# Landmark products that trail by ten steps, an attention batch that starts in the planned head, and weight work placed elsewhere

## The chip, the cores and the metric

The program runs on one core of a Trainium2 chip. TensorE (PE) does the matmuls; VectorE (DVE), ScalarE (ACT) and GpSimd (POOL) do the work between them; SyncE (SP) issues the DMAs. The metric is the device time of one execution in microseconds; the median of the runs shown counts.

## The reference

Attention is approximated with 32 landmarks for each head (means over 18 neighbouring tokens), and two dense layers follow:

```python
# q, k, v: (4 batches, 8 heads, 576 tokens, 64)
q_lm, k_lm = means of q and k over groups of 18 tokens
A, Bm, C = sm(q, k_lm), sm(q_lm, k_lm), sm(q_lm, k)
Z = Bm^T / (norms);  six times: Z = 2 * Z - Z @ Bm @ Z
x = A @ Z @ C @ v                      # then as 2304 x 512
h = x @ w_in;  x = (h * sigmoid(h)) @ w_out           # layer 1, d_ff 2048
h = x @ w_in2; out = (h * tanh(log1p(exp(h)))) @ w_out2   # layer 2
```

The four weight matrices come as float64; the kernel turns them into float32 on the chip. A product of float32 quality is made of three matmuls: each operand is split into a rounded part (hi) and a rest (lo), and hi*hi, hi*lo and lo*hi are added up.

## The kernel before, in words

**Landmark products.** Attention's last factor is never formed. For each batch a small matrix `wt` (from Z, C and v) is multiplied with w_in: eight landmark products `u_steps(b, jp)`, each for two of the 16 column tiles of w_in. Then h = uw x ath, where `ath`, `atl` are the parts of the softmax of the queries.

**The head.** Batch 0 and 1's attention, the conversion of layer 1's weights, layer 1 of batch 0 (`h_stream`, `y_stream`) and the landmark products of batch 1 are generators. The planner `interleave` orders them: each step has costs by engine, dependencies and a delay, and the step with the lowest beginning plus delay goes next. What it orders is issued in that order on every engine; later code can fill gaps. `y_stream` has two turns over the 16 row tiles of w_out; in the second one `wsplit_stream(j)` may split tile j into hi and lo (an ACT copy at line 794 and a DVE subtraction at line 797), with a delay of 7.32.

**The loop over layer 1.** 96 steps t follow: i from 2 to 7 (halves of batches 1 to 3, 288 tokens) and j from 0 to 15. A step has six h matmuls, the SiLU (tanh on ACT, product on DVE, hi on ACT, lo on POOL at line 662) and, two steps later, twelve y matmuls. Between them `advance` takes steps of the attention of the batch to come, 2 x 2.4 in a step of i = 2 and 2 x 1.8 later (`RA`, `RB`). That attention has to be complete at j = 1 of a batch's second half; then one landmark product follows every other step. `convert2` makes float32 of layer 2's weights and stores them in DRAM, one tile every other step from t = 0 (a load, a clip on POOL, two ACT and two DVE operations, a store). The scheduler under the kernel follows this order as a priority and takes ready work from later steps where an engine is free.

**The last half and layer 2.** From t = 80 the first tokens of layer 2 are loaded, and from t = 84 `second_weights` loads and splits its weights, one tile of each matrix in a step: ACT copies hi, DVE subtracts (line 605). Twelve turns of each lie in layer 1, six in the first steps of layer 2, where POOL subtracts. The lo parts of w_in2 go into the tiles `g0` to `g7`, which hold the landmark products until the last half has read them. A step of layer 2 is twelve hh matmuls of 384 columns and nine o matmuls of 512; six DVE operations of Mish lie between (`z` at lines 1025 to 1028), ACT's exponentials and POOL's lo part (line 1032).

**Banks.** PSUM has eight: y uses 0 to 3, h 5 and 4 in turn, attention and landmark products of the loop 6 and 7.

Of the kernel before, what the change touches and what calls it, by code (L numbers as in the profile page):

```python
# [9 lines left out]
F32R = mybir.dt.float32r  # L10
# [9 lines left out]
P = 128  # L20
# [3 lines left out]
RA = 2.4  # L24
RB = 1.8
# [19 lines left out]
def interleave(streams, done):  # L45
# [4 lines left out]
    for gen, enter, delay in streams:  # L50
        enter()
        step = next(gen, None)
        if step is not None:
            live.append([delay, gen, enter, step, 0.0])
    while live:
        best = None
        for s in live:
            step = s[3]
            if any(d not in done for d in step.deps):
                continue  # L60
            t = max([s[4]] + [done[d] for d in step.deps])
            begin, idle = None, 0.0
            for e, c in step.cost:
                at = max(t, free.get(e, 0.0))
                if begin is None:
                    begin = at
                else:
                    idle += max(0.0, at - max(begin, free.get(e, 0.0)))
                t = at + c + LATENCY
            score = (t if begin is None else begin) + WASTE * idle + s[0]  # L70
            if best is None or score < best[0]:
                best = (score, s, t)
        assert best, [(s[0], s[3].deps) for s in live]
        _, s, _ = best
        step = s[3]
        t = max([s[4]] + [done[d] for d in step.deps])
        for e, c in step.cost:
            t = max(t, free.get(e, 0.0)) + c
            free[e] = t
            t += LATENCY  # L80
        s[4] = t
        if step.key is not None:
            done[step.key] = t + (DMA_LATENCY if step.key[0] in LOADED else 0.0)
        s[2]()
        s[3] = next(s[1], None)
        if s[3] is None:
            live.remove(s)
# [3 lines left out]
def nystrom_moe_kernel(ctx, tc, q, k, v, w1i, w1o, w2i, w2o, out):  # L91
# [6 lines left out]
    M = 32  # L98
# [379 lines left out]
    def attn_softmax(st):  # L478
# [3 lines left out]
        perm = b not in dve_tr  # L482
        eng, on, c = (pool, "pool", 1.3) if perm else (dve, "dve", 0.7)
# [5 lines left out]
        yield Step([(on, c)])  # L489
        eng.tensor_tensor(ta, ta, mx[:, 0][:, :, None].to_broadcast([P, G, M]), op=ALU.subtract)  # L490
# [6 lines left out]
        yield Step([(on, c)])  # L497
        eng.tensor_tensor(ta, ta, mx[:, 2][:, :, None].to_broadcast([P, G, M]), op=ALU.mult)
# [212 lines left out]
    def attn_batch(b):  # L711
        for g in range(2):
# [150 lines left out]
    streams += [(u_steps(1, jp), Banks((3, 7)[jp % 2]), 1.24) for jp in range(NF // 2)]  # L863
    streams += [(wsplit_stream(j), Banks(), 7.32) for j in range(NF)]
# [3 lines left out]
    cur[0] = Banks(6, 7)  # L868
# [24 lines left out]
    cv2 = convert2() if is64 else iter(())  # L893

# [23 lines left out]
    def second_weights(which):  # L918
# [3 lines left out]
        for n in range(NF + 2):  # L922
# [9 lines left out]
            if n >= 2:  # L932
                j = n - 2
                raw = pend.pop(j)
                if which == 0:
                    hi = wp.tile([P, ND, P], F32R, tag=f"wc{j}", name=f"wi2h{j}")
                    if j % 2 == 0:
                        los = wp.tile([P, 2, ND, P], F32R, tag=f"g{j // 2}", name=f"wi2l{j}")
                    lo = los[:, j % 2]
# [21 lines left out]
    bg.append(attn_batch(2))  # L961
    for t in range(len(steps)):
        i, j = steps[t]
        b, hf = i // 2, i % 2
        if hf == 1 and b + 1 < B and j == 1:
            while bg:
                advance()
        if hf == 1 and j == 10 and b + 2 < B:
            bg.append(attn_batch(b + 2))
# [5 lines left out]
        hb = bank(5 - t % 2, f"h{t}")  # L975
# [3 lines left out]
        if hf == 1 and b + 1 < B and j % 2:  # L979
            u_all(b + 1, j // 2)  # L980
        advance(RA if i == 2 else RB)
        if t % 2 == 0 and i < nblk - 1:
            next(cv2, None)
        if i == nblk - 1:
# [4 lines left out]
            if j == 4:  # L989
                wgen = [second_weights(0), second_weights(1)]  # L990
            if j >= 4:
                next(wgen[0], None)
# [3 lines left out]
        advance(RA if i == 2 else RB)  # L996
# [160 lines left out]
```

## Time and profile before

| what | value |
| --- | --- |
| median of 3 runs | 908.48 us (908.18 to 911.49) |
| profiled execution, its time | 903.28 us |
| its span, first to last instruction | 901.5 us |
| PE busy | 858.0 us (95%) |
| DVE, ACT, POOL busy | 652.5, 473.0, 290.5 us |
| head, to the first h of the loop | 187.7 us |
| loop over layer 1 | 187.7 to 482.5 us |
| layer 2 | 482.5 to 901.5 us |

Line numbers (L610) are those of the kernel before. PEclk is the granted share of TensorE's clock: 1.00 is 2.4 GHz, and the lower level is 1.2 GHz. L610 is the helper that issues h, y and hh matmuls, told apart by the tile that they write.

### The profile page before, as it was taken

How to read it: one execution, taken by the hardware profiler on the slowest of the kernel's cores; microseconds unless marked ns; L12 is line 12 of the kernel's file. 1: busy time of each engine (PE TensorE's matmuls, PEld its weight loads, DVE VectorE, ACT ScalarE, POOL GpSimd, SP SyncE). 2: the span in 40 equal slices, each digit the busy share in tenths (PEclk: the TensorE clock that was granted, in tenths of full speed). 3: DMA queues.
4: the chain of work that ended last, by engine and by line, in shares of the span. 5: the costliest groups of instructions: out<-in, count | busy, mean ns of one | idle time of the engine just before them, and what ended most of it. 6: DMA issues, size and time to landing. Idle time of an engine off the chain costs nothing.

```text
span 901.5 us, 15046 instructions
## 1 busy us (share of the span) xinstructions
PE 858.0 (95%) x5440; PEld 756.1 (84%) x5440; DVE 652.5 (72%) x1267; ACT 473.0 (52%) x1013; POOL 290.5 (32%) x332
## 2 busy tenths in 40 slices
PE   7699989969999999999999899999999999999997
PEld 5467767759899898999998789899899999989896
DVE  4888867378795849832365997787787787797776
ACT  4656553255553636644365555555554554555544
POOL 2311332014333435434334742242242242242221
PEclk9999999988999999999999999999999999999999
DMA  8545664405565363713072310110110110000000
GB/s 240 157 124 167 179 185 110 106 26 157 154 195 147 95 185 119 269 41 94 26 202 71 101 53 1 36 35 1 36 36 1 36 37 1 35 1 1 36 1 35
DMA packets 95354, 79.62 MB, mean 88 GB/s; under 512 B 52528, under 2 KB 80688, under 8 KB 95280
## 3 DMA queue, kind: packets, MB, share of 16 engines
q1 hardware_dynamic: 95280, 78.67, 30.9%
q8 instruction: 42, 0.69, 0.3%
q14 instruction: 32, 0.26, 0.1%
HBM read 60.82 MB, written 17.83 MB: 87 GB/s over the span
## 4 chain that ended last, share of the span: by engine, by line
PE 76%; DVE 10%; DMA 4%; ACT 4%; issue 3%; POOL 2%; SPq 1%; ACTq 0%; DVEq 0%; POOLq 0%
PE hh L610 21%; PE o L1088 20%; PE y L610 13%; PE h L610 6%; PE ya L829 5%; PE u L533 3%; PE ha L630 3%; DMA k<-in_k_dram 1%; PE cv L374 1%; DVE z L1026 1%; DVE wl L797 1%; DVE z L1028 1%; DMA rawt<-in_moe_w_out_dram 1%; PE nw L423 1%; POOL g L662 1%
## 5 line engine op out<-in xcount | busy, mean ns | idle before, releaser
L1032 POOL TENSOR_TENSOR g<-z,g 128x384 fp32r<-128x384 f32 x94 | 96.0, 1022 | 253.0 <-ACT g L1029 251.2
L1088 PE MATMUL o<-wh,g 128*128 128x512 f32 x576 | 166.4, 396 | 8.2 <-ACT g L1029 6.7
L610 PE MATMUL y<-g,wh 128*128 128x288 f32 x768 | 163.3, 303 | 0.6 <-ACT yo L682 0.5
L662 POOL TENSOR_TENSOR g<-g,g 128x288 fp32r<-128x288 f32 x96 | 82.0, 854 | 183.8 <-ACT g L661 142.8
L1088 PEld LDWEIGHTS o<-wh,g 128*128 128x128 f32 x576 | 106.0, 188 | 29.6 <-ACT g L1029 9.8
L610 PEld LDWEIGHTS y<-g,wh 128*128 128x128 f32 x768 | 125.3, 191 | 5.8 <-issue 4.0
L610 PE MATMUL hh<-yh,wi2l 128*128 128x384 f32 x384 | 129.3, 337 | 0.0
L610 PE MATMUL hh<-yh,wi2h 128*128 128x384 f32 x384 | 129.1, 336 | 0.0
L610 PE MATMUL hh<-yl,wi2h 128*128 128x384 f32 x384 | 128.9, 336 | 0.0
L1029 ACT CAST g<-z 128x384 fp32r<-128x384 f32 x96 | 49.3, 514 | 136.3 <-DVE z L1028 136.3
L610 PE MATMUL y<-g,wl 128*128 128x288 f32 x384 | 114.7, 299 | 0.0
L1015 DVE TENSOR_SCALAR e<-hh 128x384 f32<-128x384 f32 x96 | 53.4, 557 | 64.8 <-PE hh L610 64.3
L610 PE MATMUL h<-ath,uw 128*128 128x288 f32 x384 | 94.0, 299 | 5.4 <-DVE g L660 5.4
L660 DVE SCALAR_TENSOR_TENSOR g<-th,h 128x288 f32<-128x288 f32 x96 | 43.1, 449 | 71.1 <-ACT th L659 64.6
L1088 PE MATMUL o<-wl,g 128*128 128x512 f32 x288 | 81.9, 391 | 0.0
L1016 ACT ACTIVATE e<-e 128x384 f32<-128x384 f32 x96 | 50.3, 524 | 51.6 <-DVE e L1015 51.5
L610 PEld LDWEIGHTS hh<-yh,wi2h 128*128 128x128 f32 x384 | 72.1, 188 | 3.9
L610 PEld LDWEIGHTS hh<-yl,wi2h 128*128 128x128 f32 x384 | 72.1, 188 | 3.8
L610 PEld LDWEIGHTS y<-g,wl 128*128 128x128 f32 x384 | 73.3, 191 | 0.6 <-issue 0.6
L1026 DVE SCALAR_TENSOR_TENSOR z<-z,r 128x384 f32<-128x384 f32 x96 | 71.1, 740 | 3.3
L610 PEld LDWEIGHTS h<-ath,uw 128*128 128x128 f32 x384 | 67.8, 190 | 6.7 <-DVE g L660 5.9
L610 PEld LDWEIGHTS hh<-yh,wi2l 128*128 128x128 f32 x384 | 72.1, 188 | 0.0
(168 smaller groups left out, 1611.8 us busy)
## 6 DMA issues: line engine op xcount, KB each, us to landing
rawi<-in_moe_w_in_dram SPq DMA_DIRECT2D x16, 512.0 KB, 5.3
rawo<-in_moe_w_out_dram SPq DMA_DIRECT2D x16, 512.0 KB, 3.9
rawt<-in_moe_w_in_dram SPq DMA_DIRECT2D x16, 512.0 KB, 5.1
w2c<-ct SPq DMA_DIRECT2D x32, 256.0 KB, 3.1
rawt<-in_moe_w_out_dram SPq DMA_DIRECT2D x16, 512.0 KB, 4.8
w2r<-w2c SPq DMA_DIRECT2D x32, 256.0 KB, 2.9
v<-in_v_dram SPq DMA_DIRECT2D x32, 144.0 KB, 3.8
ysc<-yo SPq DMA_DIRECT2D x32, 144.0 KB, 1.9
```

The lines of the kernel that those rows point to most:

```text
L533: pe.matmul(ub[64 * p : 64 * p + 64, jj, g], wt[:, p].rearrange("a h m -> a (h m)"), wc[2 * jp + jj][:, (2 * g + p) * P : (2 * g + p + 1) ...
L610: pe.matmul(o, a, b_, start=first and i == 0, stop=last and i == n - 1)
L630: pe.matmul(hb[:, :HB], uw[j // 2][:, j % 2, g], ath[0][:, g, hf * HB : (hf + 1) * HB], start=g == 0, stop=g == 1)
L660: dve.scalar_tensor_tensor(g2, th, 1.0, hb[:, :HB], op0=ALU.add, op1=ALU.mult)
L662: eng.tensor_tensor(gl, g2, gh.bitcast(F32), op=ALU.subtract)
L829: pe.matmul(yb[hf, m][:, :HB], wof[j][:, m * P : (m + 1) * P], gst[j // 2][:, j % 2, hf], start=j == 0, stop=j == NF - 1,)
L1015: dve.tensor_scalar(e, h, 20.0, None, op0=ALU.min)
L1016: ins = act.activation(e, e, AF.Exp)
L1026: dve.scalar_tensor_tensor(z, z, -2.0, r, op0=ALU.add, op1=ALU.mult)
L1029: act.copy(gh, z)
L1032: eng.tensor_tensor(gl, z, gh.bitcast(F32), op=ALU.subtract)
L1088: pe.matmul(obank[i][c], a[:, c * P : (c + 1) * P], w, start=j == 0 and k == 0, stop=j == NF - 1 and k == 2,)
```

## The change

Softmax of the queries of batches 2 and 3 subtracts and multiplies on POOL, as batches 0 and 1 already did, and no longer on DVE. The attention of batch 2 becomes a spare stream of the planner (delay 8.0), which ends when all other streams are done; what is left goes on in the loop. All of the loop advances 2 x 1.35 steps of attention; it has to be complete at j = 11 of a batch's second half, and the landmark products trail by ten steps: three in the second half of the batch before, five in the first half of the batch that uses them. The splits of w_out have a delay of 2.0. `convert2` starts at t = 14, makes 18 turns up to t = 63 and 16 in the 16 steps after. `second_weights(0)` starts at t = 80 with 5 turns in 4 steps, and 11 of its lo parts get tiles of their own. Banks: h 4 and 6, attention and landmark products 5 and 7, products of batch 1 in 3 and 4.

```diff
--- before.py
+++ after.py
@@ -21,8 +21,8 @@
 PT = 96
 HB = 288
 NC = 6
-RA = 2.4
-RB = 1.8
+RB = 1.35
+SHIFT = 10
 NB2 = 384
 LAG = 2
 LAG2 = 2
@@ -47,12 +47,12 @@
 
     free = {}
     live = []
-    for gen, enter, delay in streams:
+    for gen, enter, delay, *spare in streams:
         enter()
         step = next(gen, None)
         if step is not None:
-            live.append([delay, gen, enter, step, 0.0])
-    while live:
+            live.append([delay, gen, enter, step, 0.0, bool(spare)])
+    while not all(s[5] for s in live):
         best = None
         for s in live:
             step = s[3]
@@ -479,23 +479,21 @@
 
         b, g = st["b"], st["g"]
         u = f"{b}{g}"
-        perm = b not in dve_tr
-        eng, on, c = (pool, "pool", 1.3) if perm else (dve, "dve", 0.7)
         yield Step([("dve", 0.75)], [("ta", b, g)])
         taf = st["ta"]
         ta = taf.rearrange("a (c l) -> a c l", l=M)
         mx = ap.tile([P, 3, G], F32, tag="mx", bufs=2, name=f"mx{u}")
         dve.tensor_reduce(mx[:, 0], ta, axis=AX.X, op=ALU.max)
-        yield Step([(on, c)])
-        eng.tensor_tensor(ta, ta, mx[:, 0][:, :, None].to_broadcast([P, G, M]), op=ALU.subtract)
+        yield Step([("pool", 1.3)])
+        pool.tensor_tensor(ta, ta, mx[:, 0][:, :, None].to_broadcast([P, G, M]), op=ALU.subtract)
         yield Step([("act", 0.68)])
         act.activation(ta, ta, AF.Exp)
         yield Step([("dve", 1.2)])
         dve.tensor_reduce(mx[:, 1], ta, axis=AX.X, op=ALU.add)
         dve.tensor_scalar(mx[:, 1], mx[:, 1], 1e-9, None, op0=ALU.add)
         dve.reciprocal(mx[:, 2], mx[:, 1])
-        yield Step([(on, c)])
-        eng.tensor_tensor(ta, ta, mx[:, 2][:, :, None].to_broadcast([P, G, M]), op=ALU.mult)
+        yield Step([("pool", 1.3)])
+        pool.tensor_tensor(ta, ta, mx[:, 2][:, :, None].to_broadcast([P, G, M]), op=ALU.mult)
         if b == 0:
             yield Step([("dve", 0.77)], (), ("ath", 0, g))
             if 0 not in ath:
@@ -709,6 +707,8 @@
             yield step
 
     def attn_batch(b):
+        if b == 2:
+            yield Step((), [("wt", 1, 1), ("ath", 1, 1)] + [("ci", j) for j in OWN])
         for g in range(2):
             units[b, g] = new_unit(b, g)
             yield from whole_unit(units[b, g], True)
@@ -860,12 +860,14 @@
         streams += [(attn_transposes(units[1, g], ti, 4 + ti), Banks(), (0.75, 0.87)[g]) for ti in range(2)]
         streams += [(second_attention(g), a1, (0.67, 1.15)[g])]
         streams += [(attn_softmax(units[1, g]), a1, (1.36, 0.66)[g])]
-    streams += [(u_steps(1, jp), Banks((3, 7)[jp % 2]), 1.24) for jp in range(NF // 2)]
-    streams += [(wsplit_stream(j), Banks(), 7.32) for j in range(NF)]
+    streams += [(u_steps(1, jp), Banks((3, 4)[jp % 2]), 1.24) for jp in range(NF // 2)]
+    streams += [(wsplit_stream(j), Banks(), 2.0) for j in range(NF)]
+    attn2 = attn_batch(2)
+    streams += [(attn2, Banks(5, 7), 8.0, True)]
     done = {}
     with tc.manual_schedule(engines={act.engine, dve.engine, pe.engine, pool.engine, sp.engine}):
         interleave(streams, done)
-    cur[0] = Banks(6, 7)
+    cur[0] = Banks(5, 7)
 
 
     nblk = NT // HB
@@ -891,6 +893,7 @@
 
     held.append(outs[5])
     cv2 = convert2() if is64 else iter(())
+    cvn = [0]
 
     def open_second():
         rgt.close()
@@ -934,9 +937,10 @@
                 raw = pend.pop(j)
                 if which == 0:
                     hi = wp.tile([P, ND, P], F32R, tag=f"wc{j}", name=f"wi2h{j}")
-                    if j % 2 == 0:
-                        los = wp.tile([P, 2, ND, P], F32R, tag=f"g{j // 2}", name=f"wi2l{j}")
-                    lo = los[:, j % 2]
+                    if j < 11:
+                        lo = pl.tile([P, ND, P], F32R, tag=f"lo{j}", name=f"wi2l{j}")
+                    else:
+                        lo = wp.tile([P, ND, P], F32R, tag=f"g{j - 11}", name=f"wi2l{j}")
                     split(raw.rearrange("p (t f) -> p t f", t=ND), hi, lo, late.get("lo", dve))
                     win2[j] = (hi, lo)
                 else:
@@ -958,42 +962,48 @@
             y_out(ybank[i], i)
 
     steps1 = steps
-    bg.append(attn_batch(2))
+    bg.append(attn2)
     for t in range(len(steps)):
         i, j = steps[t]
         b, hf = i // 2, i % 2
-        if hf == 1 and b + 1 < B and j == 1:
+        if hf == 1 and b + 1 < B and j == SHIFT + 1:
             while bg:
                 advance()
-        if hf == 1 and j == 10 and b + 2 < B:
-            bg.append(attn_batch(b + 2))
+            if b + 2 < B:
+                bg.append(attn_batch(b + 2))
         if i == nblk - 1 and j == 0:
             for _ in cv2:
                 pass
             open_second()
             ycur, yload, ypart = y_load(0, late["pool"])
-        hb = bank(5 - t % 2, f"h{t}")
+            wgen = [second_weights(0), second_weights(1)]
+        hb = bank((4, 6)[t % 2], f"h{t}")
         h1_matmuls(hb, b, j, hf)
         gt["a", t] = gtiles(t, HB)
         silu2(hb, *gt["a", t], f"{t}", pool)
-        if hf == 1 and b + 1 < B and j % 2:
-            u_all(b + 1, j // 2)
-        advance(RA if i == 2 else RB)
-        if t % 2 == 0 and i < nblk - 1:
-            next(cv2, None)
-        if i == nblk - 1:
+        lin = NF * hf + j - NF - 1 - SHIFT
+        if lin >= 0 and lin % 2 == 0 and b + 1 < B:
+            u_all(b + 1, lin // 2)
+        lin += 2 * NF
+        if b > 1 and lin < NF and lin % 2 == 0:
+            u_all(b, lin // 2)
+        advance(RB)
+        if i < nblk - 1:
+            while cvn[0] < min(34, (18 * (t - 11) // 52 if t < 64 else t - 45)):
+                cvn[0] += 1
+                next(cv2, None)
+        else:
             if j < 4:
                 yload(j)
             elif j < 8:
                 ypart(j - 4)
-            if j == 4:
-                wgen = [second_weights(0), second_weights(1)]
+            for _ in range(1 + (j % 4 == 3)):
+                next(wgen[0], None)
             if j >= 4:
-                next(wgen[0], None)
                 next(wgen[1], None)
         if t >= LAG:
             emit_y(t - LAG)
-        advance(RA if i == 2 else RB)
+        advance(RB)
     lft.close()
```

## Rows read from the trace of the kernel before

**Rows 1.** Windows by stage: window, length, busy us (instructions) by engine, PEclk, DMA.

```profile
166.00:187.60 21.60, 21.60 (x180) 15.37 (x180) 7.92 (x15) 6.43 (x11) 0.66 (x2) 1.00 0.16 25
187.60:206.30 18.70, 11.94 (x72) 10.03 (x69) 17.47 (x35) 14.14 (x34) 3.08 (x3) 0.73 0.18 59
...
222.00:443.50 221.50, 218.24 (x1778) 204.51 (x1778) 136.98 (x297) 113.86 (x264) 87.37 (x104) 1.00 0.46 134
443.50:482.50 39.00, 38.89 (x290) 38.41 (x289) 22.49 (x38) 23.42 (x53) 13.66 (x16) 1.00 0.53 151
482.50:523.30 40.80, 34.18 (x176) 29.81 (x175) 34.55 (x44) 22.24 (x45) 25.19 (x20) 1.00 0.31 86
523.30:878.00 354.70, 354.70 (x1784) 320.41 (x1783) 283.56 (x511) 189.78 (x374) 107.40 (x105) 1.00 0.07 21
```

**Rows 2.** Timeline of DVE and of ACT behind the head's last landmark product.

```profile
188.41 0.69 DVE L550 TENSOR_TENSOR uw<-u,uw 128x512 fp32r<-128x512 f32 x1 [0.66 <-ACT uw L548]
...
188.87 8.41 ACT L794 CAST wh<-wl 128x512 fp32r<-128x512 f32 x16
197.17 0.71 ACT L659 ACTIVATE th<-h 128x288 f32<-128x288 f32 x2
```

**Rows 3.** Timeline of PE, 198 to 222: start, us, instruction, idle before and releaser.

```profile
198.91 0.61 PE L610 MATMUL h<-ath,uw 128*128 128x288 f32 x1 [5.37 <-DVE g L660]
...
203.58 0.44 PE L610 MATMUL h<-ath,uw 128*128 128x288 f32 x1
...
206.30 0.30 PE L610 MATMUL h<-ath,uw 128*128 128x288 f32 x1
...
208.68 0.29 PE L610 MATMUL h<-ath,uw 128*128 128x288 f32 x1
...
217.06 2.19 PE L374 MATMUL cv<-v,ct 96*64 96x128 f32 x24 [1.57 <-ACT ct L360]
219.18 0.85 PE L610 MATMUL y<-g,wh 128*128 128x288 f32 x2
...
221.83 0.30 PE L610 MATMUL h<-ath,uw 128*128 128x288 f32 x1
```

**Rows 4.** Timeline of PE, first hh of layer 2's third and ninth step.

```profile
489.94 0.34 PE L610 MATMUL hh<-yh,wi2h 128*128 128x384 f32 x1
...
523.33 0.34 PE L610 MATMUL hh<-yh,wi2h 128*128 128x384 f32 x1
```

**Rows 5.** Timeline of DVE and of POOL in one of these steps.

```profile
506.10 1.61 DVE L1026 SCALAR_TENSOR_TENSOR z<-z,r 128x384 f32<-128x384 f32 x1
507.75 1.55 DVE L1028 TENSOR_TENSOR z<-z,e 128x384 f32<-128x384 f32 x1
...
505.99 1.31 POOL L605 TENSOR_TENSOR wi2l<-w2r,wi2h 128x512 fp32r<-128x512 f32 x1 [0.62 <-ACT wi2h L604]
507.26 1.62 POOL L605 TENSOR_TENSOR wl<-w2r,wh 128x512 fp32r<-128x512 f32 x1
```

**Rows 6.** Tile z, one line: count, ns min/median/max, first and last start.

```profile
L1028 DVE TENSOR_TENSOR z<-z,e x96: 557/558/1553, 491.7 to 893.8; 128x384 f32<-128x384 f32 x96
```

**Rows 7.** Timeline of ACT and of POOL: one undisturbed SiLU, tanh to lo part.

```profile
318.28 0.41 ACT L659 ACTIVATE th<-h 128x288 f32<-128x288 f32 x1 [2.66 <-PE h L610]
...
319.80 0.81 POOL L662 TENSOR_TENSOR g<-g,g 128x288 fp32r<-128x288 f32 x1 [2.94 <-ACT g L661]
```

**Rows 8.** Timeline of PE: one landmark product.

```profile
303.38 1.09 PE L533 MATMUL u<-wc,wt 128*64 128x128 f32 x16
```

**Rows 9.** Timeline of DVE: conversions of layer 2's weights, first and last of eleven.

```profile
352.64 1.01 DVE L601 SCALAR_TENSOR_TENSOR ct<-rawt 128x512 uint32<-128x512 uint32 x1
...
386.01 1.19 DVE L601 SCALAR_TENSOR_TENSOR ct<-rawt 128x512 uint32<-128x512 uint32 x1
```

**Rows 10.** Tile ta: the subtraction of softmax on POOL and on DVE.

```profile
L490 POOL TENSOR_TENSOR ta<-ta,mx x4: 1157/1298/1602, 18.7 to 137.5; 128x576 f32<-128x576 f32 x4
...
L490 DVE TENSOR_TENSOR ta<-ta,mx x4: 749/796/1177, 204.8 to 343.8; 128x576 f32<-128x576 f32 x4
```

## Prediction

> **What bounds the kernel now.** I read the windows by stage first. From the loop's first undisturbed steps to the end of layer 1, PE is busy for 218.24 of 221.50 and 38.89 of 39.00 us, and then in layer 2 for all of 354.70 us [rows 1]. In these stretches nothing that the change moves on DVE, ACT or POOL can show, unless it makes PE wait: at most 3.26 + 0.11 us are to be had there. Matmul counts do not change. So I looked for the windows in which PE does wait or runs slowly. Two stand out: the beginning of the loop (11.94 of 18.70 us busy, PEclk 0.73) and the first nine steps of layer 2 (34.18 of 40.80 us) [rows 1]. The time before 166 us is not touched, since the moved splits and the spare stream both depend on work that ends at about that time.
>
> **First gap, beginning of the loop.** PE issues the first h at 187.7 us and then stops, because h of step 2 needs the bank of step 0. That bank is freed by the SiLU's product, and its tanh sits on ACT behind all 16 copies of the w_out split (188.87 to 197.17) [rows 2]; PE goes on at 198.91 after 5.37 us [rows 3]. Idle time of PE in this window: 18.70 - 11.94 = 6.76 us [rows 1]. Then it runs at the lower clock: the step from 198.91 to 203.58 takes 4.67 and the next 2.72, where the one from 206.30 to 208.68 takes 2.38 [rows 3]. That is 2.29 + 0.34 = 2.63 us. A second, smaller place follows: cv waits 1.57 us at 217.06, and the twelve y matmuls behind it take 2.65 us (219.18 to 221.83) where 12/18 of 2.38 = 1.59 is usual, 1.06 us more [rows 3]. Sum of the losses: 6.76 + 2.63 + 1.57 + 1.06 = 12.0 us.
>
> **Second gap, beginning of layer 2.** A step costs 354.70 us / 85 = 4.175 us when PE is full (1784 matmuls at 21 in a step, [rows 1]). The six steps from 489.94 to 523.33 take 33.39 us [rows 4], 5.57 each; the excess is 33.39 - 6 x 4.175 = 8.3 us. In these steps POOL subtracts two weight tiles (1.31 and 1.62 us), and in just that time DVE's two z operations take 1.61 and 1.55 us [rows 5] against a usual 0.56 [rows 6]. So about 1.0 us of DVE time is lost with each of POOL's two subtractions, and six DVE operations that need some 3.4 us need 5.5 instead, more than PE's step.
>
> **The change, part by part.**
>
> *Splits of w_out at delay 2.0.* Sixteen ACT copies at 8.41/16 = 0.53 us (8.4 us) and sixteen subtractions leave the beginning of the loop [rows 2]. They go where their inputs are read last, between 166.0 and 187.6 us. There ACT is busy for 6.43 and DVE for 7.92 of 21.60 us [rows 1]: with 8.4 more on ACT, and about 0.7 x 16 = 11.2 on DVE (as the subtraction of the same shape at 188.41 [rows 2]), it is 14.8 and 19.1 us. PE is full there and stays the bound. DVE is nearly full; without that cover the two or three last subtractions, 2 us, would trail into the loop.
>
> *New banks.* The first h now uses bank 4, which the last landmark product of batch 1 holds until its DVE subtraction ends: 188.41 + 0.69 = 189.10 in the old trace [rows 2], so h would begin 1.4 us behind 187.7. Then y of step 0 needs the whole SiLU, 318.28 to 320.61 = 2.33 us when undisturbed [rows 7]; two more h groups (2 x 2.38/3 = 1.59) cover all but 0.75. I also allow one stretch at the lower clock, 1.06 us as measured behind the 1.57 us wait [rows 3]. What is left of the 12.0 is 3.2; **gain 8.8 us**. Bounds: 12.0 if attention fills the hole; 4.7 if the 1.4 and 0.75 stay and both clock losses of the larger kind do (2 x 2.63).
>
> *Attention at 2 x 1.35, complete at j = 11; conversion from t = 14.* Batch 2's attention has 83 steps of the generator. The planner will take few, for a delay of 8 puts them behind everything until DVE lies that far behind; 27 loop steps at 2.7 take 73. Its two chains of dependent work (where cv waited) get more room, and conversions no longer load in the first steps. This is counted in the 8.8. Landmark products keep their number; they are made five steps ahead of use (over 12 us). They share banks 5 and 7 with attention for sixteen steps, not six; the most that is to be had in this stretch is the 3.26 us of waits above, and I take as much again as the loss: 0, bounds -3 and +3.
>
> *Conversions, 16 in 16 steps (t = 64 to 79).* These steps hold five landmark products of 1.09 us [rows 8]; with 16 x 2.38 us they last 43.5 us, 2.72 for a conversion. Eleven conversions stand at 352.64 to 386.01, one in 3.34 us [rows 9], while attention ran too. At that rate 16 need 53.4 us: they fit only if some run ahead of their place, as the program order allows where an engine is free. I take +0.5; bounds 0 and 53.4 - 43.5 = +9.9.
>
> *Softmax on POOL.* Eight operations of 1.30 us come to POOL and eight of 0.80 leave DVE [rows 10]. POOL has 134 of 221.5 us free [rows 1]; 10.4 us of work hide there, and cost PE up to 0.5 each (4 us) if every one makes a SiLU's lo part late. DVE's part is a doubtful relief: while POOL reads, a two-input operation on DVE stretches by 1.0 us [rows 5, 6], so eight overlaps cost up to 8.0 against 6.4 saved. It is hidden by DVE's 84 idle us [rows 1] either way: 0. The Trainium skill says the same more strictly (SBUF — State Buffer, section "Who interferes with whom"): a GpSimd operation that reads SBUF and a DVE operation with two SBUF inputs exclude each other for a whole instruction. By that rule alone the move would be a net loss of about 4 us on DVE (an estimate: eight holds of 1.30 less 6.4 saved); the trace agrees in kind, with 1.61 us for a z operation that usually takes 0.56 [rows 5, 6].
>
> *Weights of layer 2.* In before, lo parts of w_in2 had to wait for tiles that the last half still read; with eleven tiles of their own the splits can start in block 6, and the faster turns finish all 16 in layer 1. Six more splits then fall on ACT and DVE in a window where each has over 15 of 39 us free [rows 1]; even at POOL's 1.31 they need 7.9. I take +0.5 (bounds 0 and +3: their two load buffers are shared with the first tokens' and can be late). In return POOL has one subtraction in a step of layer 2's beginning, not two. One of the two stretched z operations gets its 0.56 back, 1.0 us in each of six steps; I take five of them, since PE's waits for something else than DVE stay: **gain 5.0 us**; bounds 2.5 (the one subtraction overlaps both operations in every other step) and 8.3 (none matters).
>
> **The sum.** -8.8 - 5.0 + 0.5 + 0.5 = -12.8 us. Against the profiled execution: span 901.5 to 888.7, its time 903.28 to 890.5. The median of the runs lies 5.2 us above the profiled time, and I carry that over: 908.48 - 12.8 = **895.7 us**. A change under 0.5% (4.5 us) cannot be told from none.
>
> **The rivals.**
>
> 1. *Only the first gap closes.* The two buffers of `second_weights` are also used by the first tokens, so w_in2 lags, and its late splits meet layer 2's first DVE steps. Then -8.8 + 1 and nothing gained behind: about 900.5. For it: the sharing. Against: PE lost 0.11 us in this block while twenty splits ran in it [rows 1], so it bears late ones. Chance 0.14.
> 2. *The gains are eaten.* The planner places the spare stream's transposes directly behind their loads, which it takes to cost nothing; DVE's fixed order stands still behind them and the products' banks stay taken, so the 5.37 us wait returns together with the lower clock (2.63), or conversions at their measured rate take the 9.9 us. -12.8 + 8.0 to 9.9: 903.7 to 905.6, no change. Against: a spare step's delay. Chance 0.11.
> 3. *Slower.* The conversions in block 6 leave a hole in PE in every step, 3.34 - 2.72 = 0.62 us, and several fall together, so that PE's clock drops as it did behind the 1.57 us wait. At the lower level a step takes 4.67, not 2.38 [rows 3]; over 16 steps that is +36.6, less 12.8: about 932. It decides if such holes recur while PE is granted the lower clock for most of the block; half the block would still give 914. Against it: 6.62 us of idle time in layer 2's first 40.8 us left PEclk at 1.00 [rows 1]. Chance 0.06.
>
> **How the numbers follow.** The forecast has 0.69, its own range by its bounds (not all at one end) 888 to 902. Rival 1 ends within it, rival 2 at its upper end and just above. For 8 in 10 I take 887 to 904.5. Faster by over 0.5% means under 904.0: all of forecast but a few parts in a hundred, rival 1 and a share of rival 2: 0.83. Same (904.0 to 913.0): 0.10. Slower: rival 3 and mishaps that I have not named: 0.07.
>
> **What would show it.** In the changed profile the 16 copies and subtractions should stand between 166 and 190 us among landmark products; the first h some 1.4 us behind the last product; no wait over 2 us in the loop's first steps and PEclk under 1.00 there for one short stretch at most. At layer 2's beginning POOL should have one weight subtraction in a step, one z operation near 1.6 and one near 0.56, and steps of 4.2 to 4.7 us. PE's last instruction of layer 1 should come 8 to 10 us earlier. Wrong would be: a long DVE wait on a load in the head, PE waiting for h banks or lo parts between t = 64 and 79, or steps of 5.5 us in layer 2.

## The result, and the profile after

The changed kernel takes 899.75 us (median of 4 runs, 897.20 to 900.45); beside it the kernel before took 909.99 us. The ratio is 0.9883, 95% interval 0.9851 to 0.9914. In a second series it took 898.26 us against 906.78, ratio 0.9889 (0.9857 to 0.9922). So it is faster by 1.1%, 8.5 to 10.2 us; the prediction said 12.8 us and 895.7 us, and its range, 887 to 904.5, holds the time. How the sum came about is another matter: two of its zeros cost some 4 us each, a term of half a microsecond was about 2, and the gain at the beginning of the loop was larger than I took.

The profiled execution took 899.86 us, with a span of 898.1 us. The two profiled executions differ by only 3.4 us, because that of the kernel before lies below its usual time (903.28 us; its medians in these series were 906.78 to 909.99), so I compare stages, not spans.

First the windows by stage of the kernel after: window, length, then busy us and instructions of PE, weight loads, DVE, ACT and POOL, PEclk, DMA share and GB/s.

```profile
157.50:193.00 35.50, 35.50 (x242) 26.36 (x240) 23.96 (x48) 13.51 (x29) 0.00 (x0) 1.00 0.32 63
193.00:212.00 19.00, 18.99 (x135) 16.56 (x134) 12.66 (x29) 8.96 (x24) 9.26 (x10) 1.00 0.39 100
336.00:378.00 42.00, 35.45 (x265) 33.52 (x264) 33.52 (x71) 27.24 (x65) 24.29 (x26) 0.96 0.70 229
378.00:441.00 63.00, 62.98 (x528) 60.07 (x527) 26.02 (x44) 29.56 (x67) 24.21 (x28) 1.00 0.29 95
441.00:460.00 19.00, 15.60 (x104) 15.16 (x103) 9.98 (x19) 11.53 (x27) 5.94 (x7) 0.91 0.55 158
485.30:520.50 35.20, 33.85 (x176) 29.98 (x176) 28.51 (x44) 19.14 (x39) 16.11 (x14) 1.00 0.20 58
```

Set against [rows 1], the beginning of the loop went from 11.94 of 18.70 us busy at PEclk 0.73 to 18.99 of 19.00 at 1.00, and the first eight steps of layer 2 from 40.80 to 35.20 us. But two stretches of the loop that were nearly full before now have holes: 6.55 us idle at 336 to 378, and 3.40 us at 441 to 460, both with PEclk under 1.00.

**The first gap is closed.** The splits of w_out, by line: the copies of ACT and the subtractions of DVE, with ns min/median/max and first and last start.

```profile
L794 ACT CAST wh<-wl x16: 618/622/631, 156.5 to 190.9; 128x512 fp32r<-128x512 f32 x16
L797 DVE TENSOR_TENSOR wl<-wl,wh x16: 650/681/694, 158.4 to 192.4; 128x512 fp32r<-128x512 f32 x16
```

They stood in one block behind the last landmark product before [rows 2]; now they are spread over the second turn of y, which begins at 157.5 us (the first two copies start 1 us ahead of it), and the last subtraction ends as the loop begins. PE's timeline there, against [rows 3]:

```profile
191.98 1.09 PE L531 MATMUL u<-wc,wt 128*64 128x128 f32 x16
193.01 0.40 PE L608 MATMUL h<-ath,uw 128*128 128x288 f32 x1
...
194.00 1.19 PE L465 MATMUL a<-qT,qb 128*64 128x288 f32 x8
195.12 0.40 PE L608 MATMUL h<-ath,uw 128*128 128x288 f32 x1
...
196.11 0.71 PE L307 MATMUL c<-kT,qb 128*64 128x288 f32 x4
...
198.24 0.69 PE L608 MATMUL y<-g,wh 128*128 128x288 f32 x2
```

No row has a wait: attention matmuls of batch 2 (`a`, then `c`) fill the time in which PE would have waited for the first SiLU.

**Layer 2's beginning.** The first hh of its first and of its ninth step, then the z operations by line, and one step of DVE and POOL, against [rows 4 to 6]:

```profile
485.26 0.34 PE L608 MATMUL hh<-yh,wi2h 128*128 128x384 f32 x1
...
520.46 0.34 PE L608 MATMUL hh<-yh,wi2h 128*128 128x384 f32 x1
```

```profile
L1036 DVE SCALAR_TENSOR_TENSOR z<-z,r x96: 557/558/1616, 492.9 to 889.8; 128x384 f32<-128x384 f32 x96
L1038 DVE TENSOR_TENSOR z<-z,e x96: 557/558/560, 493.5 to 890.4; 128x384 f32<-128x384 f32 x96
```

```profile
506.21 1.62 DVE L1036 SCALAR_TENSOR_TENSOR z<-z,r 128x384 f32<-128x384 f32 x1
507.86 0.56 DVE L1038 TENSOR_TENSOR z<-z,e 128x384 f32<-128x384 f32 x1
...
506.10 1.31 POOL L603 TENSOR_TENSOR wl<-w2r,wh 128x512 fp32r<-128x512 f32 x1 [0.62 <-ACT wh L602]
```

POOL has one weight subtraction in a step, beside it one z operation still takes 1.62 us, and the other one never takes more than 0.56.

**The new holes.** PE's waits of the kernel after, at 336 to 378 (three lines) and at 441 to 460 (two lines): who waited for what, us in all, times, longest.

```profile
PE nw L423 <- DVE rv L435: 3.2, 3, 2.3
PE y L608 <- DVE yo L682: 2.6, 1, 2.6
PE y L608 <- POOL g L660: 0.7, 2, 0.5
...
PE y L608 <- ACT g L659: 2.9, 1, 2.9
PE y L608 <- POOL g L660: 0.5, 1, 0.5
```

How the wait of 2.6 us at 348.92 comes about is seen in the timelines of POOL, of ACT, of DVE and of PE:

```profile
344.28 1.45 POOL L513 TENSOR_TENSOR atl<-at,ath 128x576 fp32r<-128x576 f32 x1 [0.88 <-ACT ath L511]
345.69 0.79 POOL L660 TENSOR_TENSOR g<-g,g 128x288 fp32r<-128x288 f32 x1
346.45 1.07 POOL L590 TENSOR_SCALAR rawt<-rawt 128x512 f32<-128x512 f32 x1
...
347.56 0.69 ACT L592 ACTIVATE rawt<-rawt 128x512 f32<-128x512 f32 x1 [1.79 <-POOL rawt L590]
348.12 0.41 ACT L680 ACTIVATE yo<-y 128x288 f32<-128x288 f32 x1
...
344.36 1.40 DVE L344 TENSOR_SCALAR bc<-be,rc 128x32 f32<-128x32 f32 x1
345.68 1.34 DVE L595 SCALAR_TENSOR_TENSOR rawt<-rawt 128x512 uint32<-128x512 uint32 x1
...
348.92 0.50 PE L608 MATMUL y<-g,wh 128*128 128x288 f32 x2 [2.61 <-DVE yo L682]
```

POOL is a chain of attention's lo part, a SiLU's lo part and a conversion's clip. ACT stands 1.79 us at the scaling that needs the clip, and the copy of y that frees a bank is behind it; DVE's copies of y come at 348.32 and 349.05, when two operations are through that took 1.40 and 1.34 us beside POOL's (the medians of their lines are 0.57 and 0.69). None of the three POOL operations is one that the change moved; whether those have a part in this hole is asked below.

### The profile page after: what moved, and what is told of

Same layout as the page of the kernel before. It is cut to its first block, busy times and chain, and to the rows that moved or that the text cites. A ratio compares the mean times of both kernels' runs of the same rounds, so it can differ in the third digit from the quotient of the medians.

```text
span 898.1 us, 15048 instructions
## 1 busy us (share of the span) xinstructions
PE 863.3 (96%) x5440; PEld 762.3 (85%) x5440; DVE 651.1 (73%) x1265; ACT 472.7 (53%) x1013; POOL 293.9 (33%) x334
## 4 chain that ended last, share of the span: by engine, by line
PE 79%; DVE 8%; DMA 5%; ACT 3%; POOL 2%; issue 2%; SPq 1%; ACTq 0%; DVEq 0%; POOLq 0%
PE hh L608 21%; PE o L1098 20%; PE y L608 14%; PE h L608 7%; PE ya L829 5%; PE u L531 4%; PE ha L628 3%; DMA q<-in_q_dram 2%; PE nw L423 1%; DVE z L1036 1%; DMA w2r<-w2c 1%; DMA k<-in_k_dram 1%; PE cv L374 1%; POOL rawt L590 1%; PE c L307 1%
```

## The experiments

Four more series, each beside runs of the kernel before on the same chip; ratios are to those. "Loop" is the time from the first h of step 0 to the first hh of layer 2, "hh" the first eight steps of layer 2, "head" what lies ahead of the loop, all from the profiled execution of each.

| kernel | median us | ratio to before (95%) | head | loop | PE idle in loop | hh |
| --- | --- | --- | --- | --- | --- | --- |
| before, shown above | 909.99 | | 187.7 | 294.8 | 11.7 | 40.8 |
| before again | 908.27 (one) | | 189.7 | 297.3 | 13.1 | 40.8 |
| after | 899.75 | 0.9883 (0.9851 to 0.9914) | 193.0 | 292.3 | 10.1 | 35.2 |
| after again | 898.26 | 0.9889 (0.9857 to 0.9922) | 191.1 | 293.0 | 10.5 | 35.2 |
| before + early splits | 897.09 | 0.9885 (0.9852 to 0.9918) | 194.4 | 284.3 | 2.9 | 41.3 |
| after, splits late | 911.08 | 1.0042 (1.0017 to 1.0067) | 189.1 | 307.0 | 19.7 | 35.2 |
| before + layer-2 weights | 904.51 | 0.9976 (0.9950 to 1.0001) | 189.5 | 295.7 | 13.9 | 35.1 |
| before + both | 893.16 | 0.9838 (0.9810 to 0.9866) | 192.8 | 286.1 | 3.9 | 35.1 |
| before + both + POOL softmax | 897.35 | 0.9878 (0.9849 to 0.9906) | 191.3 | 291.5 | 8.0 | 35.2 |
| after, conversions as before | 900.88 | 0.9913 (0.9887 to 0.9939) | 187.5 | 295.1 | 13.4 | 35.5 |
| after, attention faster | 898.12 | 0.9892 (0.9857 to 0.9928) | 187.8 | 293.9 | 10.4 | 35.2 |
| after, DVE softmax | 891.47 | 0.9824 (0.9788 to 0.9859) | 187.0 | 287.8 | 5.8 | 35.5 |
| after, wt kept | 896.05 | 0.9871 (0.9834 to 0.9909) | 193.8 | 288.7 | 7.4 | 35.2 |
| after, both of these | 889.70 | 0.9797 (0.9760 to 0.9833) | 190.0 | 284.5 | 4.5 | 35.2 |

### The parts alone

The kernel before, unaltered, for the spread of profiled executions:

> The kernel before, unchanged, once more. Theory: the head (to the first h of the loop) differs between executions by several us through its loads and PE's clock, so the changed kernel's head of 193.0 us against 187.7 is not the change's doing; this run's head lies anywhere between 187 and 194 us, and the loop from there to the first hh takes 294 to 296 us as before. Rival: the change itself lengthened the head; then this run shows 187.7 us again, within 1 us.

Its loop took 297.3 us, 2.5 more than in the profile shown and 1.3 above what I expected, so loops of two executions agree within about 1%, and a difference of under 2.5 us between two loops is not read. The last two stretches of 16 steps repeat within 0.6 us.

The splits alone:

```diff
-    streams += [(wsplit_stream(j), Banks(), 7.32) for j in range(NF)]
+    streams += [(wsplit_stream(j), Banks(), 2.0) for j in range(NF)]
```

> The kernel before with the delay of the w_out splits at 2.0 and nothing else. Theory: the first gap is the splits' alone, 9 to 12 us less than before (about 898 to 900), with no wait over 2 us in the loop's first 20 us. Rival: the slower attention, the later conversions and the new banks closed it; then the splits alone bring less than 4 us.

Median 897.09 us: this one number gives as much as the whole change. PE's largest wait of the loop, and then that of layer 2's beginning:

```profile
PE y L610 <- ACT yo L682: 0.7, 1, 0.7
...
PE o L1088 <- ACT g L1029: 4.3, 4, 1.2
```

The loop is 10.5 us shorter than in the first profile of the kernel before, and 13.0 than in the second. Layer 2's beginning still waits, as it should.

The reverse, all of the change without this:

```diff
-    streams += [(wsplit_stream(j), Banks(), 2.0) for j in range(NF)]
+    streams += [(wsplit_stream(j), Banks(), 7.32) for j in range(NF)]
```

> The changed kernel with the splits' delay back at 7.32. Theory: 9 to 12 us slower than the changed kernel, so about as slow as before (907 to 911), with a wait of about 5 us and a lower clock behind the head. Rival: the spare stream fills the gap, and it loses less than 4 us.

911.08 us, slower than the kernel before. The 16 copies stand in front of tanh again, and PE waits for the bank:

```profile
190.27 8.41 ACT L794 CAST wh<-wl 128x512 fp32r<-128x512 f32 x16
198.57 0.71 ACT L657 ACTIVATE th<-h 128x288 f32<-128x288 f32 x2
...
199.62 0.61 PE L608 MATMUL h<-ath,uw 128*128 128x288 f32 x1 [8.00 <-DVE g L658]
```

So everything else in the change together gives nothing, though it saves 5.6 us at layer 2's beginning: it must lose as much elsewhere. Next, layer 2's weights alone:

```diff
-                    if j % 2 == 0:
-                        los = wp.tile([P, 2, ND, P], F32R, tag=f"g{j // 2}", name=f"wi2l{j}")
-                    lo = los[:, j % 2]
+                    if j < 11:
+                        lo = pl.tile([P, ND, P], F32R, tag=f"lo{j}", name=f"wi2l{j}")
+                    else:
+                        lo = wp.tile([P, ND, P], F32R, tag=f"g{j - 11}", name=f"wi2l{j}")
...
+            wgen = [second_weights(0), second_weights(1)]
...
-            if j == 4:
-                wgen = [second_weights(0), second_weights(1)]
-            if j >= 4:
+            for _ in range(1 + (j % 4 == 3)):
                 next(wgen[0], None)
+            if j >= 4:
```

> The kernel before with only the weight work of layer 2 moved (lo tiles of their own, faster turns from j = 0). Theory A: two load buffers alone make the 3.4 us wait with its 1.7 us of lower clock that the changed kernel shows at 445 to 451 us; then layer 2's beginning gains 5.6 us, the last half loses 5, and the time is that of before within 2 us. Theory B: that wait comes from the loads beginning late (425 us, behind the later conversions); here they begin near 403 us, there is no wait over 1 us, and the time is 5 to 6 us less than before.

904.51 us. The gain at layer 2's beginning is there (35.1 us). Steps 64 to 80 took 41.2 us, 2.6 more than before, and the last 16 steps 38.3, no more than before. Theory B has the mechanism right: the first load begins at 404.16 us, and PE's longest wait from 380 us to layer 2 is 0.6 us, though ACT waits for late loads (11.1 us in 12 waits). Its 5 to 6 us did not come: the gain is 2.7, since steps 64 to 80 give back as much. So the last 5 us of the changed kernel's loss at 80 to 96 (43.8 us) come from something that this kernel does not have.

### Where the rest of the change loses

> The changed kernel with one thing put back: one conversion step behind every even step of layer 1, as in the kernel before, in place of the sparse beginning and one at every step from t = 64. Everything else of the change stays. Theory (the dense conversions stand in ACT's and DVE's order beside attention 3 and hold y_out's and SiLU's copies there, and the late conversions also keep the queue of SP from layer 2's loads): the waits of 2.61 and 2.28 us at 348 to 366 and the low clock behind them go, steps 48 to 80 fall from 102.4 us by 6 to 8, the last 16 steps from 43.8 by 2 to 4, layer 2's first eight steps stay near 35.2; 889 to 893 us, a ratio of 0.977 to 0.981 to the kernel before. Rival A (the even pace of attention or its softmax on POOL holds PE there): steps 48 to 80 stay within 2 us of 102.4, ratio 0.986 to 0.990. Rival B (the early conversions cost y_out's end of the first two blocks what they save): gain of 6 or more at 48 to 80, but 3 or more lost at 4 to 48 (136.4 us in the changed kernel).

```diff
-            while cvn[0] < min(34, (18 * (t - 11) // 52 if t < 64 else t - 45)):
-                cvn[0] += 1
+            if t % 2 == 0:
                 next(cv2, None)
```

My theory fell: 900.88 us. Steps 48 to 80 won 2.6 us (99.8 after 102.4) and the last 16 won 1.5, but steps 4 to 48 lost 8.0 (144.4 after 136.4), beside batch 2's attention: rival B, though with a smaller gain than it asked for. PE's waits at 348.92 and 364.40 are gone (its longest in steps 48 to 63 is now 1.5 us), but what that saves is lost elsewhere. And layer 2's first load still began only at 424.38 us, though the last converted tile was sent off at 382 to 386:

```profile
382.08 3.49 SPq L891 DMA_DIRECT2D w2c<-ct  x2
...
424.38 0.32 SPq L910 DMA_DIRECT2D yr<-ysc  x1
```

> The changed kernel with 1.8 background steps for each call, where the change has 1.35, so that attention 2 and 3 end earlier (attention 3 near t = 52 and not 59), ahead of most of the dense conversions; the conversions stay as changed. Theory (the loss at 338 to 378 us is attention 3 together with the dense conversions, not either alone): steps 48 to 64 fall from 57.7 us by 3 to 5, ratio 0.982 to 0.986. Rival A (the conversions alone hold ACT and DVE): no change within 2 us in steps 48 to 80, ratio 0.987 to 0.990. Rival B (a denser attention brings waits of its own in steps 32 to 48, 53.0 us in the changed kernel): those steps rise by 2 us or more.

```diff
-RB = 1.35
+RB = 1.8
```

898.12 us, no change. Steps 48 to 64 took 49.2 us and not 57.7, but 32 to 48 took 63.1 and not 53.0: the work and its waits moved together. At step 50 PE waits only 0.4 us, but 3.2 at step 46. Rival B.

> The changed kernel with the two softmax operations of batches 2 and 3 back on DVE (POOL has them in the change). Theory of the prediction (a cost of 0): ratio 0.985 to 0.991 to the kernel before, steps 32 to 64 (110.7 us in the changed kernel) within 2 us. Rival (POOL's long operations stretch DVE's in the same stretch and delay POOL's clips, and PE waits for both): steps 32 to 64 fall by 3 us or more, and ratio 0.980 to 0.984.

```diff
+        perm = b not in dve_tr
+        eng, on, c = (pool, "pool", 1.3) if perm else (dve, "dve", 0.7)
...
-        yield Step([("pool", 1.3)])
-        pool.tensor_tensor(ta, ta, mx[:, 0][:, :, None].to_broadcast([P, G, M]), op=ALU.subtract)
+        yield Step([(on, c)])
+        eng.tensor_tensor(ta, ta, mx[:, 0][:, :, None].to_broadcast([P, G, M]), op=ALU.subtract)
```

(and the same for the multiplication.) 891.47 us: the rival, not the prediction's zero. The loop is 4.5 us shorter (287.8 after 292.3), 3.7 of them in steps 48 to 64. PE's waits there, 333 to 387, and then ACT's for POOL's clips:

```profile
PE y L610 <- ACT g L661: 2.2, 1, 2.2
PE nw L423 <- DVE rv L435: 0.8, 2, 0.5
...
ACT rawt L594 <- POOL rawt L592: 3.0, 5, 1.2
```

In the changed kernel ACT's waits for the clips in these steps were 7.5 us in 8. The wait of 2.3 us for DVE at 364.40 is gone here, and PE idles 3.0 of 53.9 us where it idled 6.5 of 57.7. But the hole of step 50 (at 348.92 in the changed kernel) is not softmax's: PE waits 2.2 us in that step here too (341.51), now for ACT's g. It stands, with 2.2 to 2.6 us, in all five profiles that have the change's early splits, conversions and pace, on whichever engine softmax is. With the conversions as before, or the attention faster, PE waits under 0.5 us in that step. So the hole takes both, the conversions and the pace.

Is the price of softmax on POOL one of its own, or only in this plan? The early splits and layer 2's weights on the kernel before, without and with the softmax on POOL:

> The kernel before with two parts of the change alone: the delay of 2.0 for the splits of w_out, and the second weights of layer 2 begun at the last block with buffers of their own for their low parts. Attention, landmark products, softmax, banks and conversions are the kernel before's. Theory (the gains at both places add up, and the other parts of the change cost what the second gives): head to layer 2 as with the split alone, first eight steps of layer 2 at 35.2 and not 41.3 us, 1 to 4 us lost at steps 64 to 96; 890 to 895 us, ratio 0.980 to 0.985, 3 to 7 us under the changed kernel. Rival (the losses at the last half are as large as the gain behind it): ratio 0.987 to 0.990, as the split alone.

> The kernel before with the early splits and layer 2's weight work, as in the run of these two parts, and one more part of the change: the softmax operations of batches 2 and 3 on POOL. Attention's pace, landmark products and conversions are the kernel before's. It asks whether POOL's softmax costs something by itself. Theory (it costs only where conversions stand close together beside the end of attention 3, as in the changed kernel): the steps from 4 to 96 take 275.5 us as without it, within 1.5, ratio 0.981 to 0.986. Rival (POOL's 1.3 us operations in front of its clips and lo parts cost PE time anywhere): 2 to 5 us more in steps 4 to 64 (196.5 without it), ratio 0.986 to 0.990.

```diff
-        eng, on, c = (pool, "pool", 1.3) if perm else (dve, "dve", 0.7)
+        eng, on, c = (pool, "pool", 1.3)
```

893.16 us without, 897.35 with; the two ran in different series, and the intervals of their ratios overlap (0.9838 and 0.9878), so the profiles decide. The window from step 4 to the end of the loop, without and with (one row from each of the two profiles):

```profile
203.30:478.90 275.60, 271.69 (x2175) 255.44 (x2174) 179.85 (x380) 147.81 (x344) 108.88 (x126) 1.00 0.47 137
```

```profile
201.80:482.80 281.00, 272.99 (x2174) 257.96 (x2173) 175.59 (x373) 148.51 (x344) 119.30 (x134) 0.99 0.47 135
```

PE idles 8.0 us and not 3.9, and the window is 5.4 us longer, with the plan of conversions and attention as in the kernel before. My theory (no cost here) fell, and the rival held: steps 4 to 64 took 201.6 us after 196.6. So softmax on POOL costs by itself; DVE did get 4.3 us of its time back, and it bought nothing. PE's largest hole there (the run without it waits 0.7 us in that step) can be followed back, over POOL, ACT and PE:

```profile
206.15 1.71 POOL L498 TENSOR_TENSOR ta<-ta,mx 128x576 f32<-128x576 f32 x1
...
209.61 1.46 POOL L515 TENSOR_TENSOR atl<-at,ath 128x576 fp32r<-128x576 f32 x1 [0.80 <-ACT ath L513]
211.01 1.10 POOL L592 TENSOR_SCALAR rawt<-rawt 128x512 f32<-128x512 f32 x1
...
212.15 0.67 ACT L594 ACTIVATE rawt<-rawt 128x512 f32<-128x512 f32 x1 [1.33 <-POOL rawt L592]
...
213.23 2.08 PE L374 MATMUL cv<-v,ct 96*64 96x128 f32 x24 [2.08 <-ACT ct L360]
```

Softmax's multiplication ends at 207.86 us; its transpose (DVE, 208.06) and hi part (ACT, 208.85) follow, then POOL's lo part, and the clip stands behind that one. ACT waits 1.33 us for the clip, and the copy `ct` that PE needs is next in its order (212.72). The price measured in these pairs holds also what the scheduler orders differently when two operations change their engine.

The second loss. In the changed kernel the last landmark product and the first load of layer 2 stand like this (PE, then SP, then ACT, which waits for that load):

```profile
423.98 1.09 PE L531 MATMUL u<-wc,wt 128*64 128x128 f32 x16
...
425.15 0.32 SPq L910 DMA_DIRECT2D yr<-ysc  x1
...
429.03 0.51 ACT L914 CAST yh<-yr 128x384 fp32r<-128x384 f32 x1 [2.97 <-DMA yr<-ysc]
```

The load begins as the product ends. So it does in all twelve profiles that leave `wt` where it is, 0.1 us behind the product, the kernel before included (403.43 after 403.34 us). The tile `wt` that the products read lies in the attention pool, and layer 2's buffers take over the place of that pool. To test it, `wt` moves to a pool that lives to the end of layer 1:

```diff
-            pl, tag = (wp, f"gt{g + 1}") if b == 0 else (ap, f"wt{g}")
+            pl, tag = (wp, f"gt{g + 1}") if b == 0 else (xp, f"wt{g}")
```

> The changed kernel once more, unaltered, for a second profile of it and a ratio beside the two kernels below. Theory (the head, 193.0 us to the first product of step 0 in the profile at hand, varies from execution to execution and has nothing of the change in it): the part from there to the end repeats within 2 us (705.1), and the head may lie anywhere from 187 to 195. Rival (the early splits or the longer live tiles lengthen the head): head at 192 to 195 again. Ratio to the kernel before 0.985 to 0.992.

> The changed kernel with one change: the tiles wt of batches 1 to 3, which the landmark products read, lie in a pool that lives to the end of layer 1, and not in the attention pool whose place layer 2's loads take over. Theory (the loads of the last block wait for that place, which the last landmark product frees at 425 us; now that the products trail by ten steps, this is 20 us later than before): the first load starts at 400 to 410 us and not at 425, the wait of PE for ACT's copy near 450 goes, the last 16 steps of layer 1 fall from 43.8 to 38.5 to 41, and the kernel is 3 to 5 us faster than the changed one beside it. Rival A (the loads wait for the conversions or for their place in SP's order): start stays at 420 or later, time within 2 us. Rival B (two load buffers are the limit wherever the loads start): the start moves, but the last 32 steps (88.5 us) fall by less than 2.

> The same, with the softmax operations of batches 2 and 3 back on DVE as well. Theory (the two losses are apart, one at steps 48 to 64 and one at 80 to 96, and both go): steps 48 to 64 near 54.0, steps 80 to 96 at 38.5 to 41, 7 to 10 us under the changed kernel, ratio to the kernel before 0.977 to 0.981: 886 to 890 us where the kernel before takes 907. Rival (what one saves the other takes back): ratio 0.981 to 0.985, as with the softmax alone.

The first load goes off at 393.25 us and the last 16 steps have no hole at all:

```profile
393.25 0.32 SPq L910 DMA_DIRECT2D yr<-ysc  x1
```

```profile
444.20:482.50 38.30, 38.30 (x290) 38.30 (x289) 18.52 (x33) 20.73 (x48) 13.69 (x16) 1.00 0.38 116
```

They fell from 43.8 and 44.0 us to 38.3; steps 64 to 80 took 2.0 to 2.2 us more (46.7), since the splits now start in them. Net 3.5 us in the last 32 steps (85.0 after 88.5), and 3.6 to 4.3 in the loop. The median, 896.05, is 2.2 us lower, and the intervals of the two ratios overlap; the place of the loss is shown by the profile, its size to the microsecond is not. The load starts earlier than I expected (400 to 410), the median gains less than the 3 to 5 us. With both mended the kernel takes **889.70 us**, ratio 0.9797 (0.9760 to 0.9833): the best of all, 8.6 us under the changed kernel beside it.

**The head.** Its time in the ten profiles with early splits is 187.0 to 194.4 us (mean 190.9), in the four with late ones 187.7 to 189.7 (mean 189.0). But from the second turn of y, with which the early splits begin, to the first h of the loop it is 35.5 us in all fourteen, with PE full. This is the stretch in the kernel before, where no split stands in it; for the kernel after it is the first row of the windows above.

```profile
152.20:187.70 35.50, 35.50 (x242) 26.39 (x241) 13.99 (x33) 7.76 (x16) 1.30 (x2) 1.00 0.37 85
```

What differs lies ahead of that, so the long head in the profile shown is not the splits' work; the two profiles of the kernel before differ by 2.0 us as well.

## Why the prediction came out as it did, by its own steps

**First gap, right, mis-sized: 8.8 predicted, 10.1 to 13.0 measured.** The splits alone give 10.1 us in the medians (897.09 against 907.20) and 10.5 and 13.0 in the loops. I had left 3.2 us of the 12.0 standing: the bank 4 wait (1.4), the SiLU (0.75) and one clock loss (1.06). None is seen in the changed kernel: the first h stands right behind the last product, and the sign "some 1.4 us behind" did not come. PE had attention's matmuls for those moments and, as the order of the rows suggests (the profile leaves tile numbers out), h of step 1 in the other bank. The gain lies near the upper bound, "if attention fills the hole". The experiment with the splits alone reached it with the old banks, so the new banks earned nothing that is seen. The splits did not stand where the prediction put them: counted back from the first h, 9 of the 16 copies ran ahead of the 21.6 us of [rows 1]. So DVE, which it saw "nearly full" with 19.1 of 21.60 us, is busy 23.96 of 35.50. Two slips touch no term: the window of 34.18 of 40.80 us holds eight steps of layer 2, not nine, and by its own terms the lower bound is 4.6, not 4.7.

**Layer 2's beginning, right: 5.0 predicted, 5.6 measured** (35.2 us after 40.8), with just the rows that were named: one subtraction in a step, one z operation at 1.6 and one at 0.56 us.

**The last half, mis-sized: 0.5 predicted for the weights and 0 for the landmark products, about 2 and 3.6 to 4.3 measured.** Early weight work by itself costs 1.9 us in steps 64 to 96 (79.0 after 77.1 with early splits), within its bounds of 0 to 3. The rest is a wait that I did not see, and it lies beyond its bound of 3: the step "Landmark products keep their number; they are made five steps ahead of use" looked at who waits for the products, not at what the products hold. Trailing by ten steps, they keep the attention pool alive 20 us longer, and layer 2's first load starts at 425 and not at 400 to 404 us. The loads of weights then don't keep ahead, and in the changed kernel ACT's copies wait for them in order:

```profile
448.67 0.62 ACT L602 CAST wi2h<-w2r 128x512 fp32r<-128x512 f32 x1 [1.94 <-DMA w2r<-w2c]
...
450.89 0.51 PE L608 MATMUL y<-g,wh 128*128 128x288 f32 x2 [2.94 <-ACT g L659]
```

**Softmax on POOL, wrong: 0 predicted, 4.2 to 5.4 us of the loop measured.** Three pairs of runs agree in kind: 4.5, 4.2 and 5.4 us in the loops, 8.3, 6.4 and 4.2 in the medians (899.75 and 891.47; 896.05 and 889.70; 897.35 and 893.16). Only the second pair ran in one series, and its two intervals just miss each other. The failing step is "It is hidden by DVE's 84 idle us": idle time as a share of 221.5 us says nothing of the moment. POOL serves three chains in order, and what stands in front of a clip moves ACT and in the end PE, as the 2.08 us hole showed. I had a price for such a delay, "up to 0.5 each (4 us) if every one makes a SiLU's lo part late", and set it to nothing. For the changed kernel's own hole at 364.40, which goes with softmax, the path is open: none of the moved operations stands on POOL in the 22 us ahead of it.

Beside it I had an estimate of about 4 us by the Trainium skill (SBUF — State Buffer, section "Who interferes with whom") and let the average overrule it. One row is of that rule's kind: the conversion's two-input operation at 345.68 took 1.34 us beside POOL's 0.79 and 1.07, against a median of 0.69. But the loss did not come on DVE, as the estimate has it: its busy time in the loop fell in all three pairs, by 4.0 to 5.0 us of the 6.4 that leave it. That price and estimate have the same size is chance.

**Conversions, right in size, wrong in place.** The prediction put 16 into steps 64 to 79 and said that they fit only if some ran ahead of their place. All did: the last was sent off at 390 us, and step 64 began at 396.7. PE has no wait from 378 to 441 us (62.98 of 63.00 us busy). They met the end of attention 3 instead, and with the even pace they make the hole of step 50, which I did not see. That their late start also spares steps 4 to 48 (136.4 us, 144.4 with the conversions as before) hides it in the sum.

**Even attention, 0 predicted.** With both losses mended the loop takes 284.5 us; the kernel before with early splits 284.3, and with layer 2's weights too 286.1. So the pace, the trailing products and the conversions together are worth 1.6 us in the loop, less than one profile can tell (3.5 us in the medians, of two series with overlapping intervals).

**The balance.** From the loop with early splits alone, 284.3 us, to the changed one, 292.3, it is 8.0 us; putting softmax back on DVE and `wt` into the other pool takes 7.8 of them away (4.5 and 3.6 one at a time). The weight work and the rest cancel, within what one profile can tell. So the losses were 8.0 us and not 1.0, and the gains 15.7 to 18.6 and not 13.8; of 12.8 us 8.5 to 10.2 were left. That the total came near is luck: both sides were off. One sign that the prediction named failed with it: counted from the first h, layer 1 ended 1.8 to 5.0 us earlier, not 8 to 10. Rival 2, "The gains are eaten", was nearer in kind than its chance of 0.11 said, but through POOL and a held pool, not through the spare stream's transposes or conversions in steps 64 to 79.

## What to carry to other kernels

When work is moved later, list what it keeps alive, and see whose buffers take over that place: the price shows up as a late DMA far from the edit. An operation moved to an engine with idle time is not free when that engine serves several chains in order; price it by what stands behind it at its moment, not by the engine's share. And where a change has many parts, take each alone: here one delay was worth as much as the whole change, layer 2's weight work 4 us more, and two other parts cost 8.

## What the runs showed of the hardware that I had not expected

A tiny operation can be held as long as a large one: DVE's `bc` line (128x32) took 0.24 to 1.40 us in the changed kernel, the longest of them beside a POOL subtraction of 1.45 us. And in the changed kernel the single waits of PE of 2.6 and 2.9 us were each followed by a stretch at the lower clock (PEclk 0.91 in 336 to 354 and in 441 to 460 us), so that such a hole cost more than its idle time. The wait of 2.28 us at 364.40 was not (1.00 in 354 to 378), and at layer 2's beginning 1.35 us of idle time in 35.2 left PEclk at 1.00.
